# Attention and a gated feed-forward on one core: three visits' scaling moved to VectorE, a rounding to the visit's head, results unloaded before dealt work

## The chip, the cores and the metric

The kernel runs on one core of one Trainium2 chip, in one launch. The metric is the device time in microseconds of that core. Lower is better. "Before" and "after" are the two versions of the kernel; the numbers of lines are those of the kernel before, unless it is said otherwise.

## The reference

```
q_n = q / sqrt(mean(q*q, -1) + 1e-6) * g_q          # q, k, v: (8, 12, 448, 64), float32
k_n = k / sqrt(mean(k*k, -1) + 1e-6) * g_k
attn = softmax(q_n @ k_n.T / sqrt(64)) ;  y = attn @ v
x = y as (8*448, 12*64) = (3584, 768)
h = x @ w_in                                        # w_in (768, 2048)
g = h * sigmoid(h)
out = g @ w_out                                     # w_out (2048, 768)
```

Both weight matrices arrive in 64-bit floats, and the kernel makes rounded 32-bit floats of them on the chip.

## The kernel before, in words

**Visits.** The 96 heads (8 batches of 12) are taken four at a time, which gives NC = 24 visits, c = 0 to 23. `visit(c)` computes the scores of four heads, their exponentials and the products with v, which are finished in the next visit. `between(c)` stands after `visit(c)` and does what lies between two visits: the softmax's sums and their reciprocals, the transposes of the next q and k, the normalisation of the visit after that, and a part of the first matrix product (x times w_in). GROUP is 6, LATE 9, SOON 11.

**Products between visits.** x times w_in is done by a scheme of seven products for a two-by-two block (`Seven`). A product is six matmul records of TensorE, 128x128 by 128x448. Its result lies in a bank, mostly one of two named mm, at times one named sc, and must be unloaded before the bank can be used again: by VectorE (`plus`, recorded at L898), which adds it to an earlier result, or by ScalarE's copies (L960, L969). GpSimd adds two intermediate results (L972, L973). When both rows of a block are done ScalarE applies silu (L1096), and SP stores them to the tensor `hidden` (L988). The rows live in three buffers named stage, so a copy into one must wait for the store of what it held.

**Who deals.** `fill(others, prompt)` draws products from a generator, one matmul at a time. After each third step of a product it calls the next piece of `prompt`; the pieces of `others` are dealt out evenly over the steps. The code that unloads a product runs in the generator only when its next step is drawn. So what was dealt after the last matmul of a product stands ahead of that product's unloading in its engine's order. Each engine works in the order in which its instructions were written.

**The weights.** A piece of w_in is loaded (L88, SP), opened (two instructions of ScalarE, L103 and L104) and rounded: three of VectorE (L126, L129, L133) and an addition on GpSimd (L137), which frees the raw words for a later load. `halves` says which of these steps ("o" open, "r" round) are dealt in which half of a `between`, by the number 2 (c - 6) + half; `visits` gives those that stand within a visit, two roundings ("rr") in visits 8 and 10. `sum_w_in` then makes sums of the rounded weights (L895, L898 on W).

**q from visit 9 on.** ScalarE squares the q rows (`square`, L698), VectorE sums them (`sum_squares`, L704), TensorE adds the two halves by a matmul with a near-identity (L715, in `scale`), VectorE adds the small constant (L716), GpSimd takes the power -1/2 (L719) and multiplies the q rows by it (L722). In the next `between` VectorE transposes the rows in blocks (`flip`, L681). k has its own transpose (L685), after which ScalarE scales by the gains (`gain`, L691); its squares are L474 and its sums L475. `scale(c + 2)` stands at the end of `between(c)`, from c = 7 on.

**Within a visit.** `turn` copies one column into a bank (L756, by VectorE in these visits) between two groups of products with v; `divide` (L849) multiplies the finished products by the reciprocals; after it come `weights_in_visit` and, further on, the sums of exponentials (`add`, L794). Exponentials are L748, scores L743, products with v L780, sums of exponentials L818, reciprocals L827, their copy L833.

**SP's queue.** SP issues nearly all DMAs in the order written, among them the loads of v (L314, L325, L327), q and k, the loads of w_in and the stores of silu's rows.

Of the kernel before, what the change touches and what calls it, by code (L numbers as in the profile page):

```python
# [13 lines left out]
ALU = mybir.AluOpType  # L14
# [528 lines left out]
def bounded(  # L543
# [10 lines left out]
    NC, loads, place, norm, spare, ones, first, squares = (  # L554
        own[name] for name in ("NC", "loads", "place", "norm", "spare", "ones", "first", "squares")
    )
# [49 lines left out]
    def q_of(c):  # L606
        return rows_q[c % 2 if c < GROUP + 2 else 0]
# [87 lines left out]
    def square(c):  # L695

        if c < NC:
            nc.scalar.activation(squares, q_of(c)[:, 0 : z.NK], AF.Square)  # L698
# [10 lines left out]
    def scale(c):  # L709

        if c >= NC:
            return
        f = norm.rms[c % 2][:, 0:n]
        t = ps.tile([P, 2, BANK], F32, name="sc", bufs=2)[:, 0, 0:n]
        nc.tensor.matmul(t, ident, f, start=True, stop=True)  # L715
        nc.vector.tensor_scalar(  # L716
            out=f, in0=t, scalar1=1.0 / D, scalar2=1e-6, op0=ALU.mult, op1=ALU.add
        )
        nc.gpsimd.tensor_tensor(out=f, in0=f, in1=minus_half.to_broadcast([P, n]), op=ALU.pow)  # L719
        rows = q_of(c)[:, 0 : z.NK].rearrange("p (n e) -> p n e", e=z.Q)  # L720
        factor = f.rearrange("p (n one) -> p n one", one=1).to_broadcast([P, n, z.Q])
        nc.gpsimd.tensor_tensor(out=rows, in0=rows, in1=factor, op=ALU.mult)  # L722

    def pair_up():

# [8 lines left out]
    def scores(c, j, i=None):  # L734


        two = ps.tile([P, 2, BANK], F32, name="sc", bufs=2)
        for half in range(2):
            pair = half if j == LEFT else i
            keys = kT[:, ds((z.KA, z.KB)[0 if j == LEFT else i] + j * P, P)]  # L740
            for h in range(2):
                rows = ds(h * D, D)
                nc.tensor.matmul(  # L743
                    two[ds(half * D, D), h, 0:S], keys[rows, ts(half, D)], qT[rows, pair, :],
                    start=True, stop=True,
                )
        for h in range(2):
            nc.scalar.activation(  # L748
                left_weights(c)[:, h] if j == LEFT else weights(c, j)[:, i, h], two[:, h, 0:S], AF.Exp,
                scale=norm.column(c, i, h, j),  # L750
            )
# [167 lines left out]

    ps_alone = None  # L920
    turns = dict(next=0, aside=False, least=99, most=99)
    filler = dict(work=iter(()), due=0.0, share=0.0, ended=False)

    def bank(n):
        turn = turns["next"] = (turns["next"] + 1) % 4
# [81 lines left out]
    def sum_w_in(i, step):  # L1007

        assert room.w_in.rounded >= (i + 1) * z.NW
        summed.add((i, step))  # L1010
        w = room.chunk(i).rearrange("p (c m r k) -> p c m r k", c=z.NW, m=2, r=2)
        up, low = w[:, 0:HW], w[:, HW:]
        s = room.sums(i).rearrange("p (s c m k) -> p s c m k", s=3, c=HW, m=2)
        left_sums(
            up[:, :, :, 0], low[:, :, :, 0], up[:, :, :, 1], low[:, :, :, 1],
            s[:, 0], s[:, 1], s[:, 2], (step,),
        )
# [371 lines left out]
    def fill(others=(), prompt=()):  # L1389


        others, prompt, steps, dealt = list(others), list(prompt), 0, 0
        if prompt:
            prompt.pop(0)()
        filler["due"] += filler["share"]
        total = max(1, int(filler["due"] / S))
        while filler["due"] > 0:
            step = next(filler["work"], None)
            if step is None:
                break  # L1400
            if step == 0:
                continue
            filler["due"] -= step
            steps += 1
            if prompt and steps % HW == 0:
                prompt.pop(0)()
            while dealt < min(len(others), len(others) * steps // total):
                others[dealt]()
                dealt += 1
        if filler["ended"]:  # L1410
            next(filler["work"], None)
        filler["due"] = min(filler["due"], 0.0)
        for other in prompt + others[dealt:]:
            other()
# [15 lines left out]


    step_of = {"o": lambda: room.w_in.open(), "r": lambda: room.w_in.round()}
    halves = {0: "ro", 1: "ro", 2: "ro", 3: "roo", 4: "or", 5: "or", 6: "or", 7: "oroo"}
    visits = {GROUP + 2: "rr", GROUP + 4: "rr"}
    for c in range(GROUP // 2):
        halves[2 * (c - GROUP)], halves[2 * (c - GROUP) + 1] = "rr", "o"
# [9 lines left out]
        return work + [lambda a=a: sum_w_in(*a) for a in sums_halves.get(i, ())]  # L1446

    def weights_in_visit(c):
        for step in visits.get(c, ""):
            step_of[step]()  # L1450
        if c in sums_visits:
            for step in range(4):
                sum_w_in(sums_visits[c], step)

    def last_two(c):
# [2 lines left out]
    def visit(c):  # L1458

        beside = normalise(c + 1) if 0 < c <= GROUP else []  # L1460
        if c == GROUP:
            beside = [lambda: None] + beside[2:]
        if c < NC:
            scores(c, 0, 0)
        if c == 0:
            first_q(1)
            normalise_alone(1)
            scores(c, 1, 0)
        run_all(beside[0:1])
        if c > 0:  # L1470
            weigh(c - 1, LEFT)
            weigh(c - 1, LEFT - 1, 0)
            turn(1, nc.scalar.copy if c <= GROUP else nc.vector.tensor_copy)
            if GROUP < c < NC and c % GROUP == 0:
                sum_x(last_two(c), 0, range(2, 4))
        if c < NC:
            scores(c, 0, 1)
        if c > 0:
            weigh(c - 1, LEFT - 1, 1)
            if c - 1 < EARLY:  # L1480
                for i in range(2):
                    nc.vector.tensor_copy(x_of(c - 1, i), sums[i])
                run_all(beside[1:2])
                if c == GROUP // 2 + 1:
                    divide(c - 2, None)
                if inverting:
                    while len(inverting) > 1:
                        inverting.pop(0)()
                    if c > 1:
                        divide(c - 2, None)  # L1490
            else:
                divide(c - 1, sums)
                if c == GROUP:
                    for i in range(1, HW):
                        sum_x(last_two(c), i, range(2))
                    for i in range(2):
                        norm.scale(c + 1, q_of(c + 1), q_of(c + 1), i, nc.vector)
                    room.w_in.round()
                run_all(beside[1:2])
                if GROUP < c < NC and c % GROUP == 0:  # L1500
                    for i in range(1, HW):
                        sum_x(last_two(c), i)
                weights_in_visit(c)
            if c + 1 < NC:
                loads["vrest"](c + 1)
        if c == NC:
            return
        if c > 0:
            scores(c, 1, 0)
        scores(c, 1, 1)  # L1510
        if c <= GROUP:
            run_all(beside[2:3])
        weigh(c, 0, 1)
        scores(c, 2, 0)
        weigh(c, 1, 1)
        turn(0, nc.scalar.copy)
        if c < GROUP:
            run_all(beside[3:4])
        scores(c, 2, 1)
        weigh(c, 0, 0)  # L1520
        if c < GROUP:
            scores(c, LEFT)
        if c != GROUP - 1:
            run_all(add(c, 1))
        weigh(c, 1, 0)
        if c < GROUP // 2:
            room.w_in.open()
        if c >= GROUP:
            scores(c, LEFT)
        if c + 1 < NC:  # L1530
            loads["v"](c + 1)
        if len(inverting) == 1:
            inverting.pop()()

    def run_all(work):
        for piece in work:
            piece()

    def between(c):
# [64 lines left out]
        if c >= LATE - 2:  # L1604
            if c == LATE - 2:
                pair_up()
            queries = prompt[3:] + [lambda: sum_squares(c + 2)]
            turning = prompt[2:3] + [lambda: square(c + 2)]
            if c < SOON:
                prompt[2:3] = [lambda: run_all(turning)]  # L1610
            else:
                queries.insert(len(queries) - 1, lambda: square(c + 2))
            steps = weights_in(c, 1)
            fill(steps + [lambda: None] * len(steps), prompt[:3] + [lambda: run_all(queries)])
        else:
            fill(weights_in(c, 1) + (further[:2] if c >= GROUP else []), prompt)
# [27 lines left out]
    for c in range(NC):  # L1644
        visit(c)
        turns.update(least=5 if c >= GROUP else 99, most=10 if c < LATE - 1 else 99)
        between(c)
    turns.update(least=99)
    visit(NC)
# [225 lines left out]
```

## Time and profile before

| what | value |
|---|---|
| median of 3 runs | 1306.1 us (1306.04 to 1306.44) |
| the profiled execution's own time | 1305.99 us |
| its span, first to last instruction | 1304.2 us |
| TensorE busy | 1289.4 us, 99% |
| VectorE busy | 958.3 us, 73% |
| ScalarE busy | 502.2 us, 39% |
| GpSimd busy | 361.7 us, 28% |
| L719, power, 128x28 | 15 times, 4791 ns each |
| L722, q rows times the power, 128x896 | 15 times, 1755 ns each |
| L137 on 128x512 | 24 times, 1278 to 3025 ns |
| granted TensorE clock | 0.999 |

The span holds three stages: the visits with the first product between them, to about 660 us; the last quarter of the first product while w_out is opened and rounded, to about 850 us; and the second product, to the end. The visits 8, 9 and 10 lie at about 181, 216 and 248 us. A row of the timeline gives start, duration, engine, line and operation, the tiles written and read with their shapes, and in brackets the idle time of the engine before the row with what ended it. The sum of the durations of an engine's rows says how much work it has; only the brackets and the gaps say what a change can be worth.

### The profile page before, as it was taken

Reading aid. Unit: us, or ns where it says so; the run is one execution under the profiler, and the core shown is the slowest. Engines: PE = TensorE matmul, PEld = TensorE weight load, DVE = VectorE, ACT = ScalarE, POOL = GpSimd, SP = SyncE. Lnnn points to the kernel's source line nnn. Section 1 sums busy time; section 2 is a strip of 40 time slices with the busy share of each in tenths; the row PEclk is TensorE's granted clock in tenths of the full one; section 3 lists DMA queues with packets and bytes.
Section 4 is the critical chain, followed back from the end, with each engine's and each line's share of the span. In section 5 each row is a group of like instructions: output and inputs, shape, how many; then the busy total and the mean of one; then the engine's idle time right before and its main releaser. Section 6 shows DMA issues by size and latency. Waiting matters only on the chain.

```text
span 1304.2 us, 19861 instructions
## 1 busy us (share of the span) xinstructions
PE 1289.4 (99%) x7182; PEld 831.2 (64%) x7182; DVE 958.3 (73%) x1647; ACT 502.2 (39%) x880; POOL 361.7 (28%) x224
## 2 busy tenths in 40 slices
PE   8999999999999999999999999999999999999998
PEld 4444444444444444444444455558999999999997
DVE  6998878868655657756554786698978787878785
ACT  7867566655554555454543344310000010000000
POOL 6755454543334333333321243300000000000000
PEclk9999999999999999999999999999999999999999
DMA  9674436534344444344321457312323223131411
GB/s 228 181 196 124 108 101 177 125 92 120 89 93 92 121 93 119 88 92 92 87 70 36 164 179 250 117 61 83 103 86 97 85 94 118 61 128 52 140 39 40
DMA packets 266159, 144.14 MB, mean 111 GB/s; under 512 B 203748, under 2 KB 249956, under 8 KB 266052
## 3 DMA queue, kind: packets, MB, share of 16 engines
q1 hardware_dynamic: 265424, 141.68, 39.5%
q8 instruction: 59, 0.97, 0.3%
q0 software_dynamic: 320, 0.90, 0.2%
q14 instruction: 48, 0.39, 0.1%
q10 hardware_dynamic: 308, 0.20, 0.1%
HBM read 95.36 MB, written 41.29 MB: 105 GB/s over the span
## 4 chain that ended last, share of the span: by engine, by line
PE 80%; DVE 2%; ACT 1%; issue 0%; DVEq 0%; ACTq 0%
PE alone L1265 23%; PE mm L949 16%; PE sc L949 10%; PE mm L1265 8%; PE alone L949 7%; PE av L780 6%; PE sc L743 6%; PE alone L1303 2%; PE sc L818 1%; PE mm L1303 1%; DVE work L898 0%; ACT work L748 0%; ACT stage L1096 0%; DVE x L898 0%; DVE work L827 0%
## 5 line engine op out<-in xcount | busy, mean ns | idle before, releaser
L748 ACT ACTIVATE work<-sc,rms 128x448 f32<-128x448 f32 x318 | 181.3, 634 | 75.1 <-PE sc L743 60.8
L743 PE MATMUL sc<-work 64*64 64x448 f32 x1344 | 164.3, 543 | 2.3 <-ACT work L748 1.0
L794 DVE TENSOR_TENSOR work<-work 128x896 f32<-128x896 f32 (+1 forms) x110 | 118.5, 1108 | 49.3 <-PE av L780 48.8
L949 PE MATMUL mm<-x,W 128*128 128x448 f32 x366 | 150.6, 544 | 2.6 <-DVE stage L898 2.0
L780 PE MATMUL av<-work,rows 64*64 64x448 f32 x1272 | 151.3, 541 | 0.8 <-ACT av L756 0.5
L949 PE MATMUL mm<-sums_x,W 128*128 128x448 f32 x348 | 143.2, 543 | 0.3 <-DVE stage L898 0.3
L503 POOL TENSOR_TENSOR rms<-rms,minus_half 128x14 f32<-128x14 f32 (+4 forms) x40 | 96.4, 2412 | 134.9 <-DVE rms L499 130.5
L530 POOL DMA_DIRECT2D out_dram<-x x2 | 1.2, 592 | 443.0 <-DVE x L898 443.0
L949 PEld LDWEIGHTS mm<-x,W 128*128 128x128 f32 x366 | 67.9, 190 | 75.4 <-issue 67.3
L1265 PE MATMUL alone<-W,rows 128*128 128x192 f32 x610 | 113.0, 326 | 0.0
L949 PEld LDWEIGHTS mm<-sums_x,W 128*128 128x128 f32 x348 | 64.9, 190 | 69.5 <-issue 64.0
L780 PEld LDWEIGHTS av<-work,rows 64*64 64x64 f32 x1272 | 58.7, 132 | 68.8 <-issue 32.7
L1265 PEld LDWEIGHTS alone<-W,rows 128*128 128x128 f32 x610 | 101.5, 190 | 0.0
L949 PE MATMUL sc<-x,W 128*128 128x448 f32 x246 | 100.1, 543 | 0.0
L743 PEld LDWEIGHTS sc<-work 64*64 64x64 f32 x1344 | 54.4, 132 | 70.6 <-ACT work L748 28.6
L719 POOL TENSOR_TENSOR rms<-rms,minus_half 128x28 f32<-128x28 f32 x15 | 71.9, 4791 | 66.5 <-DVE rms L716 64.1
L972 POOL TENSOR_TENSOR parts<-parts,stage 128x448 f32<-128x448 f32 x31 | 42.1, 1359 | 148.4 <-DVE parts L898 148.1
L949 PEld LDWEIGHTS sc<-x,W 128*128 128x128 f32 x246 | 46.0, 190 | 48.9 <-issue 45.6
L1265 PE MATMUL alone<-W,work 128*128 128x192 f32 x382 | 72.2, 326 | 0.0
L1096 ACT ACTIVATE stage<-stage 128x896 f32<-128x896 f32 x63 | 57.1, 944 | 21.3 <-DVE stage L898 20.5
L1275 ACT COPY rows<-alone 128x192 f32<-128x192 f32 x33 | 10.5, 317 | 141.6 <-PE alone L1265 141.6
L1265 PEld LDWEIGHTS alone<-W,work 128*128 128x128 f32 x382 | 63.8, 190 | 0.0
(264 smaller groups left out, 2296.3 us busy)
## 6 DMA issues: line engine op xcount, KB each, us to landing
hidden<-stage SPq DMA_DIRECT2D x63, 448.0 KB, 2.9
work<-hidden SPq DMA_DIRECT2D x21, 1024.0 KB, 5.1
rows<-in_moe_w_out_dram SPq DMA_DIRECT2D x32, 384.0 KB, 3.4
W<-in_moe_w_in_dram SPq DMA_DIRECT2D x22, 512.0 KB, 5.0
x<-hidden SPq DMA_DIRECT2D x7, 1024.0 KB, 5.8
rows<-in_q_dram SPq DMA_DIRECT2D x120, 56.0 KB, 2.2
rows<-in_k_dram SPq DMA_DIRECT2D x120, 56.0 KB, 2.3
rows<-in_k_dram SPq DMA_DIRECT2D x60, 96.0 KB, 2.5
```

Source lines behind the costliest of these rows:

```text
L503: nc.gpsimd.tensor_tensor(out=t, in0=t, in1=half, op=ALU.pow)
L719: nc.gpsimd.tensor_tensor(out=f, in0=f, in1=minus_half.to_broadcast([P, n]), op=ALU.pow)
L743: nc.tensor.matmul(two[ds(half * D, D), h, 0:S], keys[rows, ts(half, D)], qT[rows, pair, :], start=True, stop=True,)
L748: nc.scalar.activation(left_weights(c)[:, h] if j == LEFT else weights(c, j)[:, i, h], two[:, h, 0:S], AF.Exp, scale=norm.column(c, i, h, j),)
L780: nc.tensor.matmul(sums[i][ds(h * D, D), :], v, w, start=(j == 0 and step == 1), stop=(j == LEFT - 1 and step == 1),)
L794: nc.vector.tensor_tensor(out=total, in0=total, in1=more, op=ALU.add)
L818: nc.tensor.matmul(t[ds(h * D + i * n, n), :], ones[:, which + i if which else 0], left_weights(c)[:, h] if which else w()[:, i, h], start ...
L949: nc.tensor.matmul(t, self.left(name, s), self.right(name, s), start=s == ends[0], stop=s == ends[1])
L972: nc.gpsimd.tensor_tensor(out=u2, in0=u2, in1=p5, op=ALU.add)
L1096: nc.scalar.activation(t, t, AF.Silu)
L1265: nc.tensor.matmul(t, x[:, i], y, start=i == ORDER[0], stop=i == ORDER[-1])
L1303: nc.tensor.matmul(o, a[:, 2 * i + m, t], right_one(name, i)[:, m], start=n == 0, stop=n == len(steps) - 1,)
```

## The change

There are five edits.

1. The multiplication of the q rows (L722) becomes a function of its own, `scale_rows`. For c above SOON, GpSimd still does it at the end of `scale(c)`. For the q rows of visits 9, 10 and 11 VectorE does it in the visit before (8, 9, 10), in `weights_in_visit`: after the visit's roundings, and in visit 9 after the first of the four steps of `sum_w_in`.
2. The first of the two roundings of visits 8 and 10 moves from `weights_in_visit` to the head of the visit, just after the first scores.
3. `fill` draws the next step of the generator when a product has just ended, before it deals from `others`: the unloading is written ahead of the dealt work. It does so in `between(6)` to `between(10)`.
4. In the second half of `between(7)`, "roo" becomes "oro".
5. From c = 11 on the squares of the q rows are called with the transpose of k, as they were in the visits before; until then they came with the piece after it.

```diff
@@ scale(c)
         nc.gpsimd.tensor_tensor(out=f, in0=f, in1=minus_half.to_broadcast([P, n]), op=ALU.pow)
+        if c > SOON:
+            scale_rows(c, nc.gpsimd)
+
+    def scale_rows(c, engine):
+
+        f = norm.rms[c % 2][:, 0:n]
         rows = q_of(c)[:, 0 : z.NK].rearrange("p (n e) -> p n e", e=z.Q)
         factor = f.rearrange("p (n one) -> p n one", one=1).to_broadcast([P, n, z.Q])
-        nc.gpsimd.tensor_tensor(out=rows, in0=rows, in1=factor, op=ALU.mult)
+        engine.tensor_tensor(out=rows, in0=rows, in1=factor, op=ALU.mult)
@@ fill
             if prompt and steps % HW == 0:
                 prompt.pop(0)()
+            if filler["ended"] and filler["eager"]:
+                next(filler["work"], None)
             while dealt < min(len(others), len(others) * steps // total):
@@
-    halves = {0: "ro", 1: "ro", 2: "ro", 3: "roo", 4: "or", 5: "or", 6: "or", 7: "oroo"}
+    halves = {0: "ro", 1: "ro", 2: "ro", 3: "oro", 4: "or", 5: "or", 6: "or", 7: "oroo"}
@@
     def weights_in_visit(c):
-        for step in visits.get(c, ""):
+        for step in visits.get(c, "")[1:]:
             step_of[step]()
+        rows = [lambda: scale_rows(c + 1, nc.vector)] if LATE - 1 <= c < SOON else []
         if c in sums_visits:
-            for step in range(4):
+            sum_w_in(sums_visits[c], 0)
+        run_all(rows)
+        if c in sums_visits:
+            for step in range(1, 4):
                 sum_w_in(sums_visits[c], step)
@@ visit(c)
             scores(c, 0, 0)
+        for step in visits.get(c, "")[:1]:
+            step_of[step]()
@@ between(c)
             turning = prompt[2:3] + [lambda: square(c + 2)]
-            if c < SOON:
-                prompt[2:3] = [lambda: run_all(turning)]
-            else:
-                queries.insert(len(queries) - 1, lambda: square(c + 2))
+            prompt[2:3] = [lambda: run_all(turning)]
@@ the loop over the visits
         turns.update(least=5 if c >= GROUP else 99, most=10 if c < LATE - 1 else 99)
+        filler.update(eager=GROUP <= c < SOON)
         between(c)
```

More of the change, by code (lines that the diff above doesn't have):

```diff
@@ L921, in bounded @@
     turns = dict(next=0, aside=False, least=99, most=99)
-    filler = dict(work=iter(()), due=0.0, share=0.0, ended=False)
+    filler = dict(work=iter(()), due=0.0, share=0.0, ended=False, eager=False)
     def bank(n):
```

## The prediction

> **What bounds the kernel now.** I read the page first, its busy shares and the chain that ended last, then the timeline of TensorE in the stage that the change touches, and then the engine that each of its gaps names.
>
> ```profile
> span 1304.2 us, 19861 instructions
> ...
> PE 1289.4 (99%) x7182; PEld 831.2 (64%) x7182; DVE 958.3 (73%) x1647; ACT 502.2 (39%) x880; POOL 361.7 (28%) x224
> ```
>
> TensorE has work in 99% of the span and the chain gives it 80%, so an edit on another engine is worth only the gaps that it closes in TensorE's row. These are the gaps inside the change's reach (start, length, what runs, and in brackets the idle time and what ended it):
>
> ```profile
> 180.29 1.02 PE L949 MATMUL mm<-x,W 128*128 128x448 f32 x2 [0.71 <-DVE stage L898]
> ...
> 201.46 1.77 PE L949 MATMUL mm<-x,W 128*128 128x448 f32 x4 [0.58 <-DVE parts L898]
> ...
> 213.14 2.52 PE L949 MATMUL mm<-x,W 128*128 128x448 f32 x6 [1.30 <-DVE stage L898]
> ...
> 246.42 1.77 PE L949 MATMUL mm<-sums_x,W 128*128 128x448 f32 x4 [0.33 <-DVE stage L898]
> ...
> 317.48 2.03 PE L743 MATMUL sc<-work 64*64 64x448 f32 x16 [0.30 <-ACT work L748]
> ```
>
> Ends of matmuls are modelled, so I count a gap from starts. One product is six matmul records and takes 2.26 us from start to start (231.31 to 233.57 in the same timeline). By that measure the gaps cost 0.87 (A, end of visit 7's part), 0.95 (B, visit 8), 1.57 (C, end of visit 8's part), 0.60 (D, end of visit 9's part) and, with the 0.51 just before it, 0.86 (E, visit 12; visit 18 has the same near 518, together 1.7). That is 5.7 us in all: the most that can be won. A to D wait for VectorE to unload a product (L898) and so free its bank:
>
> ```profile
> 171.50 0.62 DVE L898 TENSOR_TENSOR parts<-mm,stage 128x448 f32<-128x448 f32 x1
> ...
> 179.61 0.62 DVE L898 TENSOR_TENSOR stage<-mm,parts 128x448 f32<-128x448 f32 x1 [1.11 <-POOL parts L972]
> ...
> 186.98 1.80 DVE L129 TENSOR_SCALAR W<-W 128x512 int32<-128x512 int32 x1
> ...
> 200.78 0.62 DVE L898 TENSOR_TENSOR parts<-mm,stage 128x448 f32<-128x448 f32 x1
> ...
> 212.47 0.62 DVE L898 TENSOR_TENSOR stage<-mm,parts 128x448 f32<-128x448 f32 x1
> ...
> 237.46 0.67 DVE L475 TENSOR_REDUCE rms<-rows 128x8 f32<-128x512 f32 x1
> 238.05 0.61 DVE L898 TENSOR_TENSOR stage<-mm,parts 128x448 f32<-128x448 f32 x1
> ```
>
> Why VectorE is late in visit 8 is in GpSimd's timeline and in the waits of SP's queue, then ScalarE's timeline:
>
> ```profile
> 181.75 4.79 POOL L719 TENSOR_TENSOR rms<-rms,minus_half 128x28 f32<-128x28 f32 x1 [1.08 <-DVE rms L716]
> 186.62 1.88 POOL L722 TENSOR_TENSOR rows<-rows,rms 128x896 f32<-128x896 f32 x1
> 189.59 1.41 POOL L137 TENSOR_TENSOR W<-W 128x512 int32<-128x512 int32 x1 [1.09 <-DVE W L133]
> ```
> ```profile
> SPq L88 <- POOL W L137: 13.6, 2, 10.9
> ```
> ```profile
> 202.37 0.53 ACT L969 COPY stage<-mm 128x448 f32<-128x448 f32 x1 [3.44 <-DMA hidden<-stage]
> ```
>
> L129 takes 0.43 us in most places; here it takes 1.80 and ends 0.28 after L722 does. And SP stands 10.9 us before the load of the next W piece (L88), until GpSimd has finished L137; behind it in the queue stand the eight v loads and the two stores of silu's rows, which issue at 199.56 though silu ended at 197.79. L969 waits for the first store's landing.
>
> **What the Trainium skill says.** "SBUF — State Buffer", Who interferes with whom: VectorE and GpSimd share one port pair as an exclusive lock, taken by a VectorE operation in a two-port mode or with two SBUF inputs; the later one blocks for the whole instruction. The trace agrees for L722, L137 and L972 (L129 stretched to 1.80, 1.40, 1.24) but not for the power L719/L503: at 86.38 and 86.83 the L126 and L129 took 0.41 and 0.43 inside an L503 that ran 84.53 to 87.89, and at 220.88 an L898 on W, two SBUF inputs, took 0.95 inside L719. "DMA: Bandwidth & Descriptors", Anatomy of one DMA: a DMA's wait is served by the issuing sequencer before dispatch; the 10.9 us on SP are that. "ScalarE: Activation LUTs", What ACT_TABLE_LOAD costs: 1283 ns for a load; this trace has 1283 too.
>
> **The change part by part.** Times are on the old trace's axis, each gap relative to the start of its own visit.
>
> *q rows on VectorE, first rounding at the head.* Visits 8, 9 and 10 lose one L722 each on GpSimd (1.7 to 1.9 us) and gain one VectorE multiply of the same 128x896 shape. Nearest row: L794, 1.08 us alone, 2.18 when L137 was in its way. In visit 8 the first rounding (L126 0.42, L129 0.43, L133 0.69, about 1.6 with starts) goes from 186.53 to behind L716 at 181.67, so to 183.3. It runs beside the power, and VectorE was idle there until 183.93 (2.26 us), so I cost it at nothing; that cover needs the power not to block (a rival below). GpSimd then does the first L137 at 186.6 to 187.9 straight after the power. The second rounding on VectorE starts at 186.53 as before, its L129 blocked until 188.2, L133 to 188.9; the multiply to 189.9. It does wait for the power (end 186.54), but is reached only later, so that wait is free; behind it stand the two sums L794 and the q transpose L681. The second L137 now shares the port with the multiply and the first L794, which I take at the long 2.18: L681 can start at 193.0, against 195.03. In visit 9 the multiply costs 1.08, but L895, blocked to 2.34 by L722 where its neighbours take 0.95, gives back 1.39: VectorE 0.3 earlier, nothing waits. Visit 10 is as visit 8 without a gap to close: nothing.
>
> *Gap B.* From 193.0: L681, two L794, L898 (product 2 ends 196.2), two L794, so the L898 of 200.78 ends near 199.7 instead of 201.40. TensorE could have gone on at 200.72: B closes, **-0.95**.
>
> *Gap C.* On SP the first L88 issues at 187.9, the second after 191.1; the eight v loads took 4.9 us and end near 196.4; the stores can go with silu at 197.0, 2.5 us sooner, and the first lands near 199.9. Then L969 waits for its product only (200.8). From L969 hang L474, L475, L474, L475, L827 twice, L833, L898, L685: that whole chain moves up by 1.4 to 1.5 us (202.37 to about 200.9), L685 ends near 209.6. Now the unloading stands ahead of the dealt rounding (1.6 us): L898 ends near 210.2 rather than 213.09. TensorE wants that bank at 210.7, because B is gone: C closes as well. The square sum L704, now behind the rounding, ends near 212.7, and the matmul L715 that needs it comes at 212.96, where it came at 215.50. **B and C together -2.5.** Without SP's gain the chain stays: L898 ends 211.67, then rounding and L704 to 214.2, L715 at 214.3: -1.2. These are the two ends.
>
> *Gap A.* In visit 7's part the L898 of 171.50 moves between the two L475, into 0.59 us in which VectorE waited for ScalarE's second square; both L827, the rounding, GpSimd's L137 and L972 and the L898 of 179.61 follow about 0.5 earlier. **-0.5** (0 to -0.87). The swapped open and round of that part leave the order of every engine as it was: nothing.
>
> *Gap D.* In visit 9's part the same edit does harm. L898 (238.05) now stands ahead of the first L475 (237.46), where it used to fill the wait for the second square. L475, ScalarE's square, L475, L827, L833, the rounding, L685 and the unloading that TensorE waits for all slip by its 0.6: **+0.6** (0 to +0.9).
>
> *q squares one product sooner.* From visit 11 on, L698 stands ahead of L691 in ScalarE's order; nothing else moves.
>
> ```profile
> 310.45 0.93 ACT L698 ACTIVATE rows<-rows 128x896 f32<-128x896 f32 x1
> 313.07 1.79 ACT L1096 ACTIVATE stage<-stage 128x896 f32<-128x896 f32 x2 [1.68 <-DVE stage L898]
> ...
> 316.28 4.50 ACT L748 ACTIVATE work<-sc,rms 128x448 f32<-128x448 f32 x8
> ```
> ```profile
> 311.42 1.09 DVE L704 TENSOR_REDUCE rms<-rows 128x28 f32<-128x896 f32 x1 [1.44 <-ACT rows L698]
> ```
>
> ScalarE is idle from 306.71 to 309.50, and its q rows' loads were issued by 297.9, so L698 fits there. L704 then follows L685's neighbour at 310.0 and L898 on the sc bank goes when GpSimd's L972 is done (311.26) instead of at 312.42. Silu's first half is 1.1 sooner, the second waits for the last product (312.95): table load and exponentials start 0.35 sooner. Gap E shrinks by that in two visits: **-0.7** (0 to -1.7). In the other visits no gap hangs on it.
>
> **Sum:** -0.5 -2.5 +0.6 -0.7 = -3.1. The profiled execution took 1305.99 us by its own time (span 1304.2), 0.1 below the median of 1306.1; 1305.99 - 3.1 = **1302.9**. What a measurement of this kernel can tell from no change is about 0.2%, 2.6 us: the line lies at 1303.5, close to the forecast.
>
> **Rivals.**
> (1) *SP's queue is not the cause, or the stores stay late for another reason.* For it: two of the v loads' own waits are not visible behind L88. Then B and C give -1.2, the sum is -1.8: 1304.2, no measurable change. Chance 0.24.
> (2) *More closes than I count*: A whole (-0.87), E whole (-1.7), D's slip hidden by a sooner second square (0), with -2.5: 1300.9. Chance 0.15.
> (3) *The power holds the port pair, as the skill's wording has it.* Then in visits 8 and 10 the first rounding's L129 waits at the head until 186.8, L133 ends 187.5, and behind it stands L756, which fills a column of TensorE's bank at 183.93: 3.6 us late, and TensorE waits for it before its next weighing. Twice that is +7.2, against -1.8 for the rest (A, E, D and the short -1.2): about 1311.4, slower. It decides once each head loses over 0.9 us, and is measurable from 2.2. The three operations inside powers speak against it. Chance 0.06.
>
> **Chances.** The likeliest case (0.55) lies between 1302.0 and 1304.2, four fifths of it under 1303.5: 0.44 faster, 0.11 same. With (2) 0.59 faster, with (1) 0.35 same, 0.06 slower. Leaving out (3) and about half of (2), the range is 1301.2 to 1305.0.
>
> **What would show it.** Right: no gaps near 200 and 211 (old axis); SP's wait at L88 down from 10.9 to some 7; L969 waiting for TensorE and not for a store; the first rounding at visits' heads in about 1.6 us; the D gap grown to about 1.2; ScalarE's first L748 of visits 12 and 18 about 2.7 us after TensorE's first scores instead of 3.1. Wrong: a new wait of TensorE for L756, or for L704 at L715; the multiply over 2.2 us; a span within 1.5 us of the old one with C still open.

## The result, and the profile after

The changed kernel takes **1303.14 us** (median of 13 runs, 1302.77 to 1303.47); the kernel before, run beside it, takes 1306.3 us (13 runs, 1305.81 to 1309.13). The ratio is 0.9973, with a 95% interval of 0.9965 to 0.9982. The profiled execution took 1303.14 us by its own time, against 1305.99 before: 2.85 less.

The page of the changed kernel, first the span and then the busy times:

```profile
span 1301.3 us, 19847 instructions
...
PE 1289.3 (99%) x7182; PEld 831.3 (64%) x7182; DVE 955.8 (73%) x1650; ACT 503.7 (39%) x880; POOL 357.1 (27%) x221
```

TensorE's work is unchanged (1289.4 before), so the 2.9 us of span came out of its gaps. To find which, I aligned TensorE's rows of the two traces group by group and noted each place where the shift between them changes. Line numbers past L719 are larger in the changed kernel (L898 is L904, L949 is L955, L715 stays).

| place | predicted | shift in the traces |
|---|---|---|
| A, end of visit 7's part | -0.5 | -0.52 |
| B and C, visit 8 and the end of its part | -2.5 | -0.86 and -1.57, together -2.43 |
| D, end of visit 9's part | +0.6 | +0.53 |
| F, first scores of visit 10 | not in the sum | +0.54 |
| q squares sooner, fifth edit | -0.7, through E in visits 12 and 18 | -0.84: -0.21 each at the first scores of visits 12, 15, 18 and 21 |

Together -2.72, where the aligned end moved by -2.81. TensorE's timeline after (start, length, what runs; in brackets the idle time before it and what ended it):

```profile
179.76 1.02 PE L955 MATMUL mm<-x,W 128*128 128x448 f32 x2 [0.19 <-DVE stage L904]
...
195.67 4.67 PE L955 MATMUL mm<-sums_x,W 128*128 128x448 f32 x12
200.18 1.67 PE L955 MATMUL mm<-x,W 128*128 128x448 f32 x4
...
208.03 4.67 PE L955 MATMUL mm<-x,W 128*128 128x448 f32 x12
212.54 0.30 PE L715 MATMUL sc<-rms,ident 128*128 128x28 f32 x2
...
243.99 1.77 PE L955 MATMUL mm<-sums_x,W 128*128 128x448 f32 x4 [0.85 <-DVE stage L904]
...
246.37 0.98 PE L749 MATMUL sc<-work 64*64 64x448 f32 x8 [0.47 <-ACT work L691]
```

Twelve records in a row (195.67 to 200.18, and 208.03 to 212.54) are 4.51 us, twice a product of 2.26: B and C are gone. A has shrunk, D has grown, and the last row is a wait that the kernel before did not have.

### The profile page after: what moved, and what is told of

It reads as the page before. It is cut to its first block, busy times and chain, and to the rows that moved or that the text cites. A ratio compares the mean times of both kernels' runs of the same rounds, so it can differ in the third digit from the quotient of the medians.

```text
span 1301.3 us, 19847 instructions
## 1 busy us (share of the span) xinstructions
PE 1289.3 (99%) x7182; PEld 831.3 (64%) x7182; DVE 955.8 (73%) x1650; ACT 503.7 (39%) x880; POOL 357.1 (27%) x221
## 4 chain that ended last, share of the span: by engine, by line
PE 94%; ACT 2%; DVE 2%; issue 1%; DMA 0%; SPq 0%; POOL 0%; ACTq 0%; DVEq 0%; POOLq 0%
PE alone L1271 23%; PE mm L955 19%; PE sc L955 11%; PE av L786 10%; PE sc L749 10%; PE mm L1271 8%; PE alone L955 7%; PE alone L1309 2%; PE sc L824 1%; PE mm L824 1%; PE mm L1309 1%; PE sc L642 1%; PE sc L673 0%; DMA rows<-in_k_dram 0%; ACT work L754 0%
## 5 line engine op out<-in xcount | busy, mean ns | idle before, releaser
L955 PE MATMUL mm<-x,W 128*128 128x448 f32 x366 | 150.2, 543 | 0.2 <-DVE stage L904 0.2
L955 PE MATMUL mm<-sums_x,W 128*128 128x448 f32 x348 | 143.2, 543 | 0.9 <-DVE stage L904 0.9
L955 PEld LDWEIGHTS mm<-x,W 128*128 128x128 f32 x366 | 68.1, 190 | 72.3 <-issue 67.5
L955 PEld LDWEIGHTS mm<-sums_x,W 128*128 128x128 f32 x348 | 64.9, 190 | 70.0 <-issue 64.8
L955 PE MATMUL sc<-x,W 128*128 128x448 f32 x246 | 100.1, 543 | 0.0
L719 POOL TENSOR_TENSOR rms<-rms,minus_half 128x28 f32<-128x28 f32 x15 | 72.1, 4806 | 64.9 <-DVE rms L716 64.9
L978 POOL TENSOR_TENSOR parts<-parts,stage 128x448 f32<-128x448 f32 x31 | 42.3, 1363 | 152.7 <-DVE parts L904 152.2
L955 PEld LDWEIGHTS sc<-x,W 128*128 128x128 f32 x246 | 46.0, 190 | 48.9 <-issue 45.4
```

Source lines behind the costliest of these rows:

```text
L955: nc.tensor.matmul(t, self.left(name, s), self.right(name, s), start=s == ends[0], stop=s == ends[1])
L978: nc.gpsimd.tensor_tensor(out=u2, in0=u2, in1=p5, op=ALU.add)
```

## The experiments

All times are medians; shifts are read from aligned traces, as above. "Before" is the kernel before and "changed" the changed one. The kernel before ran beside each group of runs: it took 1306.42 us beside e1 to e4, 1306.61 beside e5, e6, e7 and e9, and 1306.85 beside e10, so medians of different groups are compared by their ratios. A single shift is no evidence by itself: e3's trace has one of +0.35 us at 278, in a part that its edit does not reach. The main readings below rest on shifts that come back in several traces.

| run | median (runs) | ratio to before, 95% |
|---|---|---|
| changed | 1303.14 (13) | 0.9973 [0.9965, 0.9982] |
| e1, before with the third edit alone | 1305.69 (13) | 0.9995 [0.9987, 1.0003] |
| e2, changed without the third edit | 1303.66 (12) | 0.9977 [0.9968, 0.9986] |
| e3, before with the fifth edit alone | 1305.52 (13) | 0.9993 [0.9985, 1.0002] |
| e4, changed without the third edit in visit 9's part | 1302.28 (7) | 0.9970 [0.9958, 0.9981] |
| e5, changed without the second edit | 1303.78 (13) | 0.9978 [0.9970, 0.9986] |
| e6, changed without the first edit | 1303.23 (8) | 0.9973 [0.9962, 0.9983] |
| e7, before with SP's two loads later | 1305.46 (12) | 0.9991 [0.9983, 1.0000] |
| e9, e4 with roundings dealt later | 1303.42 (11) | 0.9976 [0.9967, 0.9985] |
| e10, e4 with one rounding and one opening placed | 1302.29 (5) | 0.9961 [0.9948, 0.9975] |

### The third edit alone, and all but the third

e1 adds to the kernel before only the unloading ahead of the dealt work; e2 takes only that from the changed kernel.

```diff
+            if filler["ended"] and filler["eager"]:
+                next(filler["work"], None)
             while dealt < min(len(others), len(others) * steps // total):
```
```diff
         turns.update(least=5 if c >= GROUP else 99, most=10 if c < LATE - 1 else 99)
-        filler.update(eager=GROUP <= c < SOON)
         between(c)
```

> The kernel before with the third edit alone (the unloading ahead of dealt work in the parts after visits 6 to 10). Theory, from the two traces: each gap is one edit's doing, and the unloading helps where an unload on the path stood behind dealt work and harms where the dealt work filled a wait. Gap A -0.5; B unchanged, for the L898 that it waits for has no dealt rounding ahead of it; C -1.2, because L898 goes ahead of the rounding, though the store's wait stays; D +0.5; and the first scores of visit 10 wait for L691 (F) by +0.5. Sum about -0.7 us, in the trace. Rival: the unloading brings the whole of the gain and the moved steps nothing: -2 to -3 us. Second rival: F comes from the moved q rows or the moved rounding, and is absent here.

> The changed kernel without the third edit; all the others stay. Theory: A stays as before (0), B closes (-0.75 to -0.95), C shrinks because the chain behind the store is 1.4 sooner but the rounding still stands ahead of L898 (B and C together about -1.3), D and F do not appear (0), the four visits after the squares -0.2 each. Sum about -2.1 us against before. Rival that takes the unloading for the cause of it all: no more than -0.8. If F shows here it is not the unloading's.

In e1, A moved by -0.51, D by +0.55 and F by +0.52; B stayed, and the end came 0.50 sooner. At C the wait for the bank went (-1.57), but 0.30 of it came back at L715: the square sum L704, now behind the rounding, ended at 213.56, and L715 began at 213.70. In e2, B moved by -0.85 and C by -0.55, the first scores of four visits by -0.21 each, there was no D and no F, and the end came 2.21 sooner. TensorE's timeline of e1 and then of e2, end of visit 8's part:

```profile
208.97 4.67 PE L949 MATMUL mm<-x,W 128*128 128x448 f32 x12
213.70 0.38 PE L715 MATMUL sc<-rms,ident 128*128 128x28 f32 x2
```
```profile
208.61 2.42 PE L955 MATMUL mm<-x,W 128*128 128x448 f32 x6
211.78 2.52 PE L955 MATMUL mm<-x,W 128*128 128x448 f32 x6 [0.75 <-DVE stage L904]
```

With B still open, TensorE comes to C late, and the third edit alone closes C. With B closed, C needs both. So A, D and F belong to the third edit, B to the others, and C to both. The others also keep L704 off the path: in the changed kernel it ended at 212.14, 0.40 ahead of L715. The third edit gains 1.5 to 1.8 us and gives 1.07 of it back in visit 9's part.

### The fifth edit alone

```diff
-            if c < SOON:
-                prompt[2:3] = [lambda: run_all(turning)]
-            else:
-                queries.insert(len(queries) - 1, lambda: square(c + 2))
+            prompt[2:3] = [lambda: run_all(turning)]
```

> The kernel before with the fifth edit alone (squares of the q rows one product sooner from visit 11 on). Theory after the result: the bank sc that the first scores of visits 12, 15, 18 and 21 want is unloaded sooner, 0.21 us each, -0.84 in all, and the gap E inside visits 12 and 18 hardly changes. The prediction's account: -0.35 in visits 12 and 18 alone, -0.7, E shrinking. The trace tells them apart: where TensorE's start shifts. Rival: it does nothing, 0, and the shifts come from what happened before.

Four shifts of -0.21 appeared, at 313.18, 414.39, 514.95 and 616.12 (first scores of visits 12, 15, 18 and 21), as in the changed kernel; the median is 0.9 lower than the 1306.42 of the kernel before beside it. e3's trace itself ends only 0.31 sooner, because small shifts the other way (+0.14 in the first microseconds, +0.12 at 213, +0.35 at 278), all ahead of the first place that the edit touches, take off most of the 0.84. VectorE's timeline of e3 in visit 12's neighbourhood:

```profile
310.50 1.06 DVE L704 TENSOR_REDUCE rms<-rows 128x28 f32<-128x896 f32 x1
311.89 0.62 DVE L898 TENSOR_TENSOR stage<-sc,parts 128x448 f32<-128x448 f32 x1 [0.33 <-POOL parts L972]
313.60 0.63 DVE L898 TENSOR_TENSOR stage<-mm,parts 128x448 f32<-128x448 f32 x1 [1.09 <-PE mm L949]
```

L704 no longer waits for its squares, so the unloading of an sc bank behind it waits for GpSimd alone. In the kernel before it ran from 312.42 to 313.03, and the first scores, which want an sc bank, began at 313.18. In the changed kernel it ends at 310.02, and the scores follow L715 at 311.08 after 0.23 us, where they took 0.43. That it is this bank is read from the order of the rows; no bracket names it.

### The first and the second edit

e5 puts both roundings back into `weights_in_visit`; e6 gives the q rows back to GpSimd.

```diff
-        for step in visits.get(c, "")[1:]:
+        for step in visits.get(c, ""):
             step_of[step]()
...
-        for step in visits.get(c, "")[:1]:
-            step_of[step]()
```
```diff
-        if c > SOON:
-            scale_rows(c, nc.gpsimd)
+        scale_rows(c, nc.gpsimd)
...
-        rows = [lambda: scale_rows(c + 1, nc.vector)] if LATE - 1 <= c < SOON else []
+        rows = []
```

> The changed kernel with the second edit undone: both roundings of visits 8 and 10 stand together after the reciprocals' multiplications, the q rows' product after them on VectorE. Theory (the rounding at the head is what frees VectorE and SP's queue in visit 8): VectorE reaches the q transpose L681 near 194.6 on the old axis instead of 192.6, so B closes only in part (-0.2 to -0.6 of its 0.85), and SP reaches its second load about 1.5 us later, which still lets the stores go near 198.5. C stays closed to about -1.2 to -1.5. Loss against the changed kernel 0.3 to 1.0 us, all of it between 190 and 215. Rival: the rows' move alone does it, and the loss is under 0.2.

> The changed kernel with the first edit undone: GpSimd multiplies the q rows in all visits, the other edits stay. Theory: with the first rounding at the head the product on GpSimd hides: VectorE is blocked by it once (L129 to about 188.8 instead of 187.9) and saves its own 1.08, so B and C still close, and visit 9 has 0.66 us of slack before the L898 that waits for the sc bank. Within 0.3 us of the changed kernel in the trace. Rival (the prediction counted both edits as needed for B): B opens again by 0.5 or more, and the kernel loses 0.5 to 1.5.

e5 is slower than the changed kernel: in the traces +0.38 at B, twice +0.10 behind it, +0.33 at L715, and 0.86 at the end. The unloading that frees B's bank ran at 199.82 instead of 198.70, and SP's longest wait at L88 was 9.0 us instead of 7.6. ScalarE's copy waited for a store again (201.45 instead of 200.43), and L704, at the end of that chain, ended only at 213.16, 0.15 before L715 began. TensorE in e5:

```profile
200.50 1.77 PE L955 MATMUL mm<-x,W 128*128 128x448 f32 x4 [0.21 <-DVE parts L904]
```

e6 ended 0.01 us apart from the changed kernel. GpSimd's timeline and then VectorE's, in visit 8 of e6:

```profile
186.16 1.77 POOL L727 TENSOR_TENSOR rows<-rows,rms 128x896 f32<-128x896 f32 x1
187.89 1.47 POOL L137 TENSOR_TENSOR W<-W 128x512 int32<-128x512 int32 x1
```
```profile
186.40 1.80 DVE L129 TENSOR_SCALAR W<-W 128x512 int32<-128x512 int32 x1
188.24 1.66 DVE L133 SCALAR_TENSOR_TENSOR W<-W 128x512 int32<-128x512 int32 x1
```

VectorE is held twice, first by the multiply and then by L137, but it is spared the multiply itself. In both kernels it then waits for TensorE before its next sum of exponentials, which starts at 190.49 in the changed kernel after 0.90 us of waiting and at 190.44 in e6 after 0.54. The unloading in question ran at 198.96, 0.26 later than in the changed kernel, and TensorE did not notice. Once the first rounding stands at the visit's head, it does not matter who multiplies the q rows.

e1 has neither of the two edits, so it shows each alone (it lacks the fourth and the fifth as well, which act elsewhere). Against e1, between visit 8 and the end of its part, e5, with the first edit alone, came 0.25 us sooner: -0.37 at B and +0.12 at C and L715. e6, with the second alone, came 1.14 sooner: -0.85 at B and -0.30 at L715. The changed kernel, with both, came 1.14 sooner too. The second edit does the whole work, and the first, which could do a part of it, adds nothing.

### SP's queue alone

The kernel before, with the two loads L88 of visit 8's roundings written behind the eight v loads.

```diff
-        for _ in range(2):
+        for _ in range(0 if self.hold else 2):
...
+                room.w_in.hold = c == LATE - 1
...
+        if room.w_in.hold:
+            room.w_in.hold = False
+            for _ in range(2):
+                room.w_in.load()
```

> The kernel before, with one thing moved: the two loads of w_in pieces that visit 8's roundings issue stand behind the eight v loads in SP's queue instead of ahead of them; nothing else differs on any engine. Theory (SP's stand before those loads holds the stores back, and these ScalarE's copy L969 and the chain behind it): the stores go about 2 us sooner, L969 waits for TensorE's product and runs about 1.4 sooner, gap C shrinks by about 1.3, B stays at 0.85. Rival (1) of the prediction: the queue is not the cause, C stays as it was, 0. A further loss is possible if the pieces then land late for their opening (L103 at 204.6).

C fell by only 0.63 us. Lines here are one higher than before's. SP's queue, then ScalarE, then VectorE, then TensorE:

```profile
197.03 1.17 SPq L989 DMA_DIRECT2D hidden<-stage  x2
```
```profile
201.34 0.53 ACT L970 COPY stage<-mm 128x448 f32<-128x448 f32 x1 [1.53 <-DMA hidden<-stage]
```
```profile
202.30 0.69 DVE L134 SCALAR_TENSOR_TENSOR W<-W 128x512 int32<-128x512 int32 x1
202.91 0.68 DVE L476 TENSOR_REDUCE rms<-rows 128x8 f32<-128x512 f32 x1
```
```profile
212.57 2.52 PE L950 MATMUL mm<-x,W 128*128 128x448 f32 x6 [0.68 <-DVE stage L899]
```

The stores left 2.5 us sooner (199.56 before) and ScalarE's copy came 1.03 sooner (202.37). So SP's queue did hold the copy. The copy still waited for its store, though, for the first store took 4.21 us to land here and 2.71 in the kernel before; why is not shown. And of the 1.03 only half reached the sum L476: the dealt rounding stood ahead of it on VectorE and ended about 203.0. There were two gates within half a microsecond of each other, and the changed kernel moves the second as well, because VectorE comes sooner to the unloading at B and to that rounding behind it (L126 at 199.24).

### Leaving the third edit out where it costs

```diff
-        filler.update(eager=GROUP <= c < SOON)
+        filler.update(eager=GROUP <= c < SOON and c != LATE)
```

> The changed kernel, with the unloading ahead of dealt work left out in the part after visit 9 alone. Theory: D and F are that part's doing and go back to what they were, 0.53 + 0.54 us: -1.0 to -1.1 us against the changed kernel, -3.9 against before. Rival: F is the price of the first rounding at the head of visit 10 (its L126 to L133 stand there), then only D goes back: -0.5 against the changed kernel.

Against the changed kernel D moved by -0.53 and F by -0.54. The median is 1302.28, the lowest of all (e10's is 1302.29), though one of its seven runs took 1303.84. Its trace ends 1.02 us before the changed kernel's: this version **beats both kernels**. What F is shows on ScalarE at the end of visit 9's part: first the kernel before, then the changed one, then e4.

```profile
239.72 0.66 ACT L103 ACTIVATE W<-W 128x512 int32<-128x512 uint32 x1
240.27 0.65 ACT L104 ACTIVATE W<-W 128x512 f32<-128x512 f32 x1
241.62 0.53 ACT L960 COPY stage<-sc 128x448 f32<-128x448 f32 x1 [0.69 <-PE sc L949]
...
247.11 1.03 ACT L691 ACTIVATE work<-work,gains 128x896 f32<-128x896 f32 x1
```
```profile
238.66 0.53 ACT L966 COPY stage<-sc 128x448 f32<-128x448 f32 x1 [1.28 <-PE sc L955]
239.09 0.66 ACT L103 ACTIVATE W<-W 128x512 int32<-128x512 uint32 x1
239.65 0.66 ACT L104 ACTIVATE W<-W 128x512 f32<-128x512 f32 x1
...
245.29 1.02 ACT L691 ACTIVATE work<-work,gains 128x896 f32<-128x896 f32 x1
```
```profile
238.69 0.53 ACT L966 COPY stage<-sc 128x448 f32<-128x448 f32 x1 [0.69 <-PE sc L955]
...
244.20 1.04 ACT L691 ACTIVATE work<-work,gains 128x896 f32<-128x896 f32 x1
```

An opening of W (L103, L104) stood ahead of the copy L966 and filled ScalarE's wait for TensorE. The third edit puts the copy first, so ScalarE waits idle and does the opening afterwards: the copy is no sooner (238.66 against 238.69), and what follows it on ScalarE is 1.1 late: the loading of a function table, silu, L698 and L691. In the kernel before L691 ended at 248.14 and the first scores began at 248.26: there was almost no slack to take.

### What is left in visit 9's part

e9 puts later roundings into two parts of e4; e10 puts just one rounding into VectorE's wait between L904 and L704, and one opening behind L691.

```diff
-    halves = {0: "ro", 1: "ro", 2: "ro", 3: "oro", 4: "or", 5: "or", 6: "or", 7: "oroo"}
+    halves = {0: "ro", 1: "ro", 2: "ro", 3: "oor", 4: "or", 5: "or", 6: "or", 7: "oroo"}
...
-            fill(steps + [lambda: None] * len(steps), prompt[:3] + [lambda: run_all(queries)])
+            spare_steps = [lambda: None] * len(steps)
+            if c == LATE:
+                steps, spare_steps = [steps[0], spare_steps[0], *steps[2:], steps[1]], spare_steps[1:]
+            fill(steps + spare_steps, prompt[:3] + [lambda: run_all(queries)])
```

> The changed kernel without the unloading ahead in the part after visit 9 (as in the earlier run), and with two roundings dealt later, each behind an unloading that TensorE waits for: in the second half after visit 7 the order open, open, round; in the second half after visit 9 the rounding behind the k transpose, the unloading and the square sum. Theory: what is left of A (0.35) and of D (0.6) goes, -0.9 us against the earlier run, about -4.8 against before; the product on GpSimd that held up L972 is now behind it. Rival: the roundings pushed back meet the next visit's (their GpSimd parts stand ahead of the power L719, whose product VectorE needs in the visit), and 0.3 to 1 us comes back as a later q transpose.

This one missed; the end came 1.3 us later than e4's. In visit 7's part the rounding met GpSimd's additions. VectorE and then GpSimd in e9:

```profile
176.21 1.24 DVE L129 TENSOR_SCALAR W<-W 128x512 int32<-128x512 int32 x1
177.48 1.50 DVE L133 SCALAR_TENSOR_TENSOR W<-W 128x512 int32<-128x512 int32 x1
```
```profile
176.01 1.15 POOL L978 TENSOR_TENSOR parts<-parts,stage 128x448 f32<-128x448 f32 x1 [0.39 <-DVE parts L904]
177.13 1.31 POOL L979 TENSOR_TENSOR stage<-parts,stage 128x448 f32<-128x448 f32 x1
```

Against e4, A came back with +0.68. In visit 9's part D closed (-0.59), and TensorE came sooner to scores whose L691 was not sooner: the first scores waited 0.55, and a late L762 cost 0.49.

```diff
+            dealt = steps + [lambda: None] * len(steps)
+            if c == LATE:
+                queries.insert(0, dealt[1])
+                dealt[1] = dealt[-1]
+                dealt.insert(6, dealt.pop(3))
-            fill(steps + [lambda: None] * len(steps), prompt[:3] + [lambda: run_all(queries)])
+            fill(dealt, prompt[:3] + [lambda: run_all(queries)])
```

> The changed kernel without the unloading ahead in visit 9's part, and in that part the second rounding of W put between VectorE's unloading L904 and L704 (where VectorE waits for ScalarE's L698), and the third opening L103/L104 put behind ScalarE's L691. If the first scores of visit 10 are late only because L691 is, and the 0.6 us at the end of visit 9's part is only the rounding that stood ahead of L904, then the gap at L955 before visit 9's last product goes (-0.6) and the first scores start without a wait since L691 comes about 1 us sooner: about -0.6 us against the changed kernel without the unloading ahead there, some 4.4 us under the kernel before. Rival: another wait takes its place, because GpSimd's rounding L137 comes later and holds up VectorE's L126 or L704 and with it the next closing of a part: 0 to +0.5 us.

TensorE's timeline of e4 and then of e10, end of visit 9's part:

```profile
240.75 2.42 PE L955 MATMUL mm<-sums_x,W 128*128 128x448 f32 x6
243.49 1.77 PE L955 MATMUL mm<-sums_x,W 128*128 128x448 f32 x4 [0.33 <-DVE stage L904]
245.10 0.30 PE L715 MATMUL sc<-rms,ident 128*128 128x28 f32 x2
245.33 0.98 PE L749 MATMUL sc<-work 64*64 64x448 f32 x8
```
```profile
241.26 3.92 PE L955 MATMUL mm<-sums_x,W 128*128 128x448 f32 x10
245.09 0.38 PE L715 MATMUL sc<-rms,ident 128*128 128x28 f32 x2
245.40 0.98 PE L749 MATMUL sc<-work 64*64 64x448 f32 x8
```

In e10 the ten records are unbroken and the gap is gone (-0.59), and the scores do not wait, because L691 is done in time (it ended at 244.62). But L715 now comes 0.14 late, behind L704, which ended at 244.95, so the scores gain 0.45. The mechanism is shown. The time is not: e10's median equals e4's, and in its profiled execution the first microseconds, which no edit touches, came 0.50 later at 9.33 and hid the gain. Against the kernel before beside it e10 is 4.56 us lower and e4 4.14, but five and seven runs that each spread over 0.7 us or more do not settle 0.45.

## Why the prediction was right, and where it was not

**The sum.** Predicted was 1302.9 us; 1303.14 is 0.24 away. That it came so near is in part luck, for two errors partly cancelled: F (+0.54) was missing, and the fifth edit gave 0.14 more than expected.

**B and C were right in size and cause.** VectorE, in visit 8 of the changed kernel:

```profile
181.06 0.42 DVE L126 TENSOR_SCALAR W<-W 128x512 f32<-128x512 f32 x1
181.51 0.43 DVE L129 TENSOR_SCALAR W<-W 128x512 int32<-128x512 int32 x1
181.97 0.69 DVE L133 SCALAR_TENSOR_TENSOR W<-W 128x512 int32<-128x512 int32 x1
...
188.50 1.08 DVE L728 TENSOR_TENSOR rows<-rows,rms 128x896 f32<-128x896 f32 x1
...
198.70 0.62 DVE L904 TENSOR_TENSOR parts<-mm,stage 128x448 f32<-128x448 f32 x1
...
209.04 0.58 DVE L904 TENSOR_TENSOR stage<-mm,parts 128x448 f32<-128x448 f32 x1
```

The head takes 1.6 us, as predicted; the multiply took its nearest row's 1.08. One term came out right by luck. The prediction took the first sum of exponentials behind the multiply at 2.18, held up by L137. It was not stretched, nor was the multiply; GpSimd's L137, begun at 188.71 beside the multiply, took 2.02 instead. But VectorE then waited 0.90 us for TensorE, so L681 started at 192.60, which is 193.13 on the old axis, where 193.0 was said. SP's waits, and ScalarE's copy:

```profile
SPq L88 <- POOL W L137: 10.3, 2, 7.6
```
```profile
200.43 0.53 ACT L975 COPY stage<-mm 128x448 f32<-128x448 f32 x1 [2.05 <-PE mm L955]
```

The longest wait at L88 fell from 10.9 to 7.6 (some 7 was said), and the copy waits for its product, not for a store. Rival (1), for which B and C would have given 1.2, fell with that, and e7 shows the queue's effect by itself. The prediction was too simple in one point: it hung the chain on SP alone, while e7 shows VectorE's rounding as a second gate 0.5 us behind it. Both moved, so the sum held. And the first edit, described as part of B's gain, contributed nothing beside the second. The prediction had also named a wait for L704 at L715 as a sign of being wrong: the changed kernel does not have it in visit 8's part, but e1 and e5 do, as L715 begins 0.14 and 0.15 us after L704 ends.

**Rival (3), the power as a lock, is refuted.** Of the three operations of the rounding at the head, L126 began 0.16 us before the power, and L129 and L133 ran at 0.43 and 0.69 us wholly inside it:

```profile
181.22 4.91 POOL L719 TENSOR_TENSOR rms<-rms,minus_half 128x28 f32<-128x28 f32 x1 [1.08 <-DVE rms L716]
```

This is narrower than "SBUF — State Buffer", Who interferes with whom in the Trainium skill, which has the later engine blocked for the whole instruction; for the power the measurement decides. L133 reads two tensors, so it speaks for operations with two inputs as well. The prediction's own case of that kind does not: the L898 at 220.88 ran 0.46 us inside L719, which ended at 221.34, and the rest mostly beside L722, which began at 221.43.

**A and D were right** to within 0.1 us each: A came from the L904 now between the two L475, which start at 169.57 and 170.84, and D from the one now ahead of them, for the first L475 starts at 235.03:

```profile
170.17 0.61 DVE L904 TENSOR_TENSOR parts<-mm,stage 128x448 f32<-128x448 f32 x1
...
234.50 0.61 DVE L904 TENSOR_TENSOR stage<-mm,parts 128x448 f32<-128x448 f32 x1
```

**The step that failed is the third edit's cost in visit 9's part.** "L475, ScalarE's square, L475, L827, L833, the rounding, L685 and the unloading that TensorE waits for all slip by its 0.6" follows VectorE's chain to the next bank, and stops. The same edit also exchanged a copy and an opening on ScalarE, whose chain ends in L691, which the next scores need; that was F, as much again. Its part in rival (2) went the wrong way too: the slip was not hidden but doubled.

**The fifth edit's size was near, its place was wrong.** ScalarE's exponentials of visit 12 were to come 2.7 us after the first scores instead of 3.1; they came at 314.14, 3.06 after 311.08. Silu did end sooner, by 0.24 relative to L715, but the scores themselves moved by 0.20, so E kept 0.79 of its 0.86. The gain arose ahead of the first scores, in four visits and not in two; as far as the order of the rows tells, it comes from an sc bank that is free sooner. The prediction had seen that unloading move, from 312.42 to 311.26 on the old axis, but did not ask who wants the bank.

**The fourth edit** was costed at nothing, which fits. Beside the third edit it leaves the order on VectorE, ScalarE and GpSimd in visit 7's part as it was (e1 against the changed kernel). Without the third, in e2, it puts one opening ahead of a copy of ScalarE, and A stayed as it was. It was not run by itself.

## What to carry to other kernels

When one order serves several engines, moving a step ahead of dealt work moves it on each of them: follow the chain on every engine to the next instruction that TensorE waits for, and write down that one's slack (here 0.1 us at L691), not only the gap in view. An edit that helps in two places and hurts in a third is worth splitting: leaving it out of one part gained 1.0 us in the traces. Where a transfer and an engine arrived at the same chain within half a microsecond, taking away one of them brought only that half.

## What the runs showed of the hardware that was not expected

GpSimd's operations in these kernels differ in whether they hold up VectorE. Inside the power L719 the int32 L129 took 0.43 us (181.51, in a row of 4.91), and beside the additions L978 and L979 of e9 the same operation took 1.24 and L133 1.50. The VectorE operations that were held ended shortly after GpSimd's: L129 at 186.45 took 1.40 and ended 0.29 after the first L137 of the changed kernel's GpSimd timeline below, and L133 in e9 ended 0.54 after L979. The second L137 began 0.21 after VectorE's multiply (188.50 to 189.58); there the multiply kept its 1.08, and L137 took 2.02:

```profile
186.10 1.46 POOL L137 TENSOR_TENSOR W<-W 128x512 int32<-128x512 int32 x1
188.71 2.02 POOL L137 TENSOR_TENSOR W<-W 128x512 int32<-128x512 int32 x1 [1.15 <-ACT work L754]
```
